# Another order table for a one-core attention and two-MLP kernel

## The chip, the cores and the metric

The kernel runs on one core of a Trainium2 chip. The metric is the device time of one launch in microseconds. Three runs of the kernel before give a median of 863.54 us (862.55 to 866.36).

## What is computed

Attention with two kinds of mask (a window of 32 keys for the first four heads, every fourth key of the last 128 for the others), and then two MLPs one after the other on its result, all in float32:

```python
def _attn_ref(q, k, v):                       # 4 batches, 8 heads, 576 positions, 64 wide
    scores = (1.0 / np.sqrt(D)) * np.matmul(q, k.transpose(0, 1, 3, 2))
    ...
    scores = np.where(masks[None, :, :, :], scores, -1000000000.0)
    scores = scores - np.max(scores, axis=-1, keepdims=True)
    attn = np.exp(scores)
    attn = attn / (np.sum(attn, axis=-1, keepdims=True) + 1e-09)
    return np.matmul(attn, v)

# x: 2304 tokens x 512; w_in 512 x 2048; w_out 2048 x 512; for both layers
x = np.square(np.maximum(x @ w_in, 0.0)) @ w_out
h = x @ moe2_w_in
x = (h * (1.0 / (1.0 + np.exp(-h)))) @ moe2_w_out
```

The weights come to the chip as 64-bit numbers and are made into pairs of float32 there: a high part that TensorE multiplies in its fast form, and the low remainder. Each product is three matmuls: high with high, high with low, low with high.

## The kernel before

The whole kernel is a list of about 4,000 steps (`Op`), each a few instructions of one engine or one transfer. `Kern` makes the steps: attention by half sequence and pair of heads (`attention`), the making of the weight pairs (`weights`), sums of weight blocks for a seven-product scheme (`sums`, `sums2`), the first layer on tokens in tiles of 256 (`mlp`) and 512 (`mlp2`), and the second layer in three tiles of 768 (`strassen`). Weights that are needed again go to device memory and come back by tile (`stream`, `stream2`).

What sets the order is one table, `ORDER`, from a search made ahead of time. It is a single list over all engines. A word names a step by its number, the engine that does it (P for TensorE, V for VectorE, A for ScalarE, G for GpSimd, D for a transfer, which SyncE issues), and behind @ the place of each buffer that the step takes. F words are dummy matmuls (`fill`). `Planner.order` emits the steps in that order, so an engine does its own words in the order in which they stand, and waits at a word until what it needs is there. A place holds 256 float32 columns of a ring in on-chip memory, or a bank of the accumulators; a step that takes a place waits until everything that used the place before it is done, a transfer out of it included.

Two places matter below. One is the chain by which a 512 KB piece of a second-layer weight is loaded and split (`weights`, lines 274 to 358): load `raw` (L274); on ScalarE, VectorE or GpSimd the steps `cv` (L282, L284) and `raw` (L290, L292); on VectorE or GpSimd the bit work on `cv` (L302 to L318), the high part and the remainder; store (L348, into `w2s`). The other is, in `strassen`, the split of a hidden tile into `hl` (L1169 high part, by ScalarE; L1171 remainder, by VectorE or GpSimd; both show as lines of the helpers `copy`, L245, and `sub`, L252) ahead of the TensorE steps at L1182.

A GpSimd step also waits, by a line in `run`, for the last VectorE step ahead of it in the list that reads two buffers of on-chip memory or is marked so (`lock`).

Of the kernel before, what the change touches and what calls it, by code (L numbers as in the profile page):

```python
# [10 lines left out]
F32 = mybir.dt.float32  # L11
# [1350 lines left out]
V113 D160@76 P86@2 V76 A154 V103 V77 V112 P104@1 A78@8 V110 V97 F8@3 V87 V114 V88 A105 V130 D169@80 A89 P115@1
V139 P106@0 A116 V131 P90@3 P117@2 D177@88 A91@60 V107 V140 A93@64 A132@68 F8@1 V118 V92 A144@10 G133 V94 V119
V108 P400@3@1@72@0 D186@92 A161@2 V109@12 A141@164 V120 G146 V403 F1@2 P121@0 V402 G142 V401 D506@201 A124 A122
V410 P404@2 A145 V123 V411 A153@14 V125 G399 V412 P1238@3 V147 D203@116 A405 A162 V155 V148 A179 P406@0 V156
D211@124 A149@84 P413@1 A1239@16 V407 V150 A1240 V163 A1241@6 P1244@3 D220@128 V157 A414 A171 V164 A158@168 V408
V1242 P415@2 A1245@18 V165 A409@8 P1243 V416 V159 A1246 A166@100 V417 V418 A170@0 D424@196 P507@0@1@96@1 V167
A1247@12 A178@4 V1248 P419@3 P1250@2 V510 A422@104 G172 A187@10 D194@108 V420 V508 V512 G180 A188 V525 V421
P1249 A511 G189 V523 V521 A1251@16 D228@36 V423 A522 V173 A513 V181 P426@3@0@112@2 A509 A526 V514 A1252 G174
F9@1 A196 V428 V429 V427 A195@6 V436 P430@2 V437 A524 V438 V515 V517 A516 A175@172 V527 P439@1 V182 A431 V425  # L1370
A1253@14 V528 V190 P432@3 A440 V176 A529 P518@0 A530 V1254 P441@2 V191 A183@120 P531@1 P1255 V433 V442 A192@176
V519 V533 G184 V434 A520 V443 V435@8 A532 A205 D539@196 V444 P534@3 A213 V204@2 V197 P445@0 P1256@1 V193 A446
A448 A537@12 V449 A535 V447 A212@0 V536 V198 A1257@18 D538 A1258 P540@0@3@20@3 D450@201 V199 A1259@4 A200@28
V1260 V558 P1261 A222 G206 V541 V556 D237@40 A557 V201 A559 V543 A542 P1262@1 V554 V207 A555 A544 D168 V545 V208
A546 P452@0@3@24@0 A1263@16 V560 V547 V451 V548 A1264 V561 V214 A563 D134 V562 F1@2 F2@1 V466 G550 A549 V455
P564@2 V454 V456 A565 V453 G209@180 A566 P551@1 V463 V465 D254@76 P457@2 A552 V464 A553 V215 A221@14 P567@1 V210
A1265@8 A458 V223 D245@72 P467@0 V1266 V224 P459@3 A468 V216 A568 D572@196 P469@2 A238@12 V460 V225 A217@32
P1267 V240 A229@10 V470 V461 G218 V462@6 A570@4 A230 V471 D478@201 V569 V472 A226@184 P473@0 V231 P1274@1 V227
A476@52 A474 A246@8 V475 D288@124 V477 V232 P573@3@0@56@1 A1275@18 V241 A1276 A239 V578 D271@112 V580 G233
P480@1@2@80@2 V576 V574 A1277@2 V587 V593 A577 V591 V589 A579 V1278 A575 D262@92 V242 A581 P1279 A590 V582 V482  # L1380
A234@88 V583 G479 V484 V481 G584 A592 V483 D571 V491 D305@24 A256 P485@0 V493 V492 V494 A594 V235 A588 P585@1
P495@3 A486 V595 V248 A255@6 D279@108 V272@0 P1286@0 A586 V596 V263@10 A243@188 V257 V597 A247 V249 A496 P487@2
A1287@16 V244 A1288 P598@1 P497@3 V488 V250 A599 A1289@2 P600@0 V489 V498 V1290 A490@14 V251@96 P1291 V499 V258
A603@4 A500 D605@201 V252 P501@2 V259 P1298@1 A502 A601 V504 D638@196 A260@192 G280@8 V505 V503 A273 V274
P1268@3 V265 A1299@18 V275 D296@116 A1300 V602 V261 P606@2@1@20@3 A1269@16 A307 V1270 P1280@0 G290 D219 V624
A264 V611 V613 G282 V609 D604 A1271@2 V622 V607 A1301@12 V266 P1292@3 A612 A610 V1302 A623 V267 A1281@18 V620
P1304@2 A1282 V1272 V268@128 A1283@14 V626 A621 V276 A614 P1273 A608 V269 A627 V1284 A1293@16 A625 V615 A1294
P1285 V628 V616 A298 V617 V629 A1295@6 V630 A277@132 V289@2 P618@0 A1305@18 P639@1@36@0 V278 A1306 A281 V619
P640@3 V643 A297@4 V641 V1296 P631@0 A1307@14 V652 P1310@2 V645 A653 V291 A632 V299 A646 V654 V283 A644 P633@0
A1311@16 V300 A642 P1316@1 A1312 V284 A1313@0 V656 A634 V636@10 A655 D666@201 V1308 P1297 A285@40 V635 V647 A657  # L1390
# [285 lines left out]
```

## Time and profile before

| what | value |
|---|---|
| median of three runs | 863.54 us |
| the profiled execution, its own time | 863.25 us |
| its span, first to last instruction | 861.5 us |
| TensorE busy | 844.4 us (98%) |
| VectorE, ScalarE, GpSimd busy | 675.9, 492.3, 169.6 us |
| 16 DMA engines, busy share | 74.2% |
| mean granted TensorE clock | 0.998 of 2.4 GHz |

The span is the profiled execution's; its time is 1.75 us longer. In the lists "L936" is a line of the kernel; PE is TensorE, PEld its weight loads, DVE VectorE, ACT ScalarE, POOL GpSimd, SP or SPq SyncE, which issues all transfers. "y<-hl,sw" is what is written and read.

### The profile page before, as it was taken

How to read it: one execution, taken by the hardware profiler on the slowest of the kernel's cores; microseconds unless marked ns; L12 is line 12 of the kernel's file. 1: busy time of each engine (PE TensorE's matmuls, PEld its weight loads, DVE VectorE, ACT ScalarE, POOL GpSimd, SP SyncE). 2: the span in 40 equal slices, each digit the busy share in tenths (PEclk: the TensorE clock that was granted, in tenths of full speed). 3: DMA queues.
4: the chain of work that ended last, by engine and by line, in shares of the span. 5: the costliest groups of instructions: out<-in, count | busy, mean ns of one | idle time of the engine just before them, and what ended most of it. 6: DMA issues, size and time to landing. Idle time of an engine off the chain costs nothing.

```text
span 861.5 us, 17083 instructions
## 1 busy us (share of the span) xinstructions
PE 844.4 (98%) x6029; PEld 797.8 (93%) x6029; DVE 675.9 (78%) x1733; ACT 492.3 (57%) x1288; POOL 169.6 (20%) x188
## 2 busy tenths in 40 slices
PE   8999999999999999899999999999999999999998
PEld 6879999999888988888988999999999999999998
DVE  5999999988887677567989999798815887537874
ACT  4989889877565364413432456675535565346552
POOL 3321000122204344123110221201200011101212
PEclk9999999999999999999999999999999999999999
DMA  9385678768989877778989899986686574682641
GB/s 340 149 273 173 201 248 275 278 227 306 360 287 328 315 276 267 261 267 300 341 292 352 310 347 309 341 284 236 233 306 233 195 256 173 215 296 89 220 148 74
DMA packets 83606, 223.59 MB, mean 260 GB/s; under 512 B 8768, under 2 KB 18240, under 8 KB 83520
## 3 DMA queue, kind: packets, MB, share of 16 engines
q1 hardware_dynamic: 83520, 222.49, 74.2%
q8 instruction: 48, 0.79, 0.4%
q14 instruction: 38, 0.31, 0.1%
HBM read 172.13 MB, written 50.33 MB: 258 GB/s over the span
## 4 chain that ended last, share of the span: by engine, by line
PE 84%; DMA 6%; DVE 4%; ACT 2%; issue 1%; POOL 1%; SPq 1%; ACTq 0%; POOLq 0%; DVEq 0%
PE y L1094 17%; PE sa L1182 14%; PE s L936 11%; PE y L1182 5%; PE y L991 4%; PE y L990 4%; PE y L992 4%; PE sa L1094 4%; PE s L788 2%; DMA w2s<-st 2%; PE ax L533 2%; PE s L790 2%; PE s L789 2%; PE y L836 2%; PE ax L625 2%; PE y L837 2%
## 5 line engine op out<-in xcount | busy, mean ns | idle before, releaser
L245 ACT CAST hl<-gq 128x384 fp32r<-128x384 f32 x168 | 79.0, 513 | 67.5 <-PE sa L1182 24.9
L1094 PE MATMUL y<-xs,ws 128*128 128x384 f32 x552 | 107.3, 334 | 0.0
L252 DVE TENSOR_TENSOR hl<-gq,hl 128x384 fp32r<-128x384 f32 x149 | 82.4, 581 | 23.2 <-ACT hl L245 22.5
L1094 PEld LDWEIGHTS y<-xs,ws 128*128 128x128 f32 x552 | 96.7, 188 | 0.1
L936 PE MATMUL s<-x,ws 128*128 128x256 f32 x576 | 78.5, 287 | 2.6 <-ACT ap L245 2.6
L1182 PE MATMUL sa<-hl,wp 128*128 128x384 f32 x432 | 79.6, 334 | 0.0
L936 PEld LDWEIGHTS s<-x,ws 128*128 128x128 f32 x576 | 74.1, 193 | 4.7 <-ACT ap L245 2.8
L991 PE MATMUL y<-g,w 128*128 128x512 f32 x192 | 75.4, 393 | 1.0 <-POOL g L252 1.0
L990 PE MATMUL y<-g,w 128*128 128x512 f32 x192 | 75.7, 394 | 0.0
L1182 PEld LDWEIGHTS sa<-hl,wp 128*128 128x128 f32 x432 | 75.3, 188 | 0.0
L992 PE MATMUL y<-g,w 128*128 128x512 f32 x192 | 74.9, 390 | 0.0
L1070 ACT COPY gq<-y 128x384 f32<-128x384 f32 x92 | 42.1, 478 | 55.4 <-PE y L1094 44.4
L952 DVE TENSOR_TENSOR h<-s,h 128x512 f32<-128x512 f32 x96 | 59.6, 620 | 17.3 <-PE s L936 9.8
L566 ACT ACTIVATE ap<-ap,ast 96x128 f32<-96x128 f32 (+3 forms) x168 | 62.2, 372 | 14.6 <-DVE ast L558 14.1
L245 ACT CAST g<-r 128x256 fp32r<-128x256 f32 (+1 forms) x82 | 41.1, 506 | 47.5 <-DVE r L972 27.3
L1065 DVE TENSOR_TENSOR gq<-y,gq 128x384 f32<-128x384 f32 x46 | 25.0, 553 | 47.8 <-PE y L1094 46.5
L252 POOL TENSOR_TENSOR hl<-gq,hl 128x384 fp32r<-128x384 f32 x19 | 24.5, 1297 | 190.4 <-ACT hl L245 124.1
L1133 DVE TENSOR_TENSOR gq<-gq,sg 128x768 f32<-128x768 f32 x48 | 47.6, 1004 | 12.0 <-ACT sg L1131 11.5
L788 PE MATMUL s<-x,w 128*128 128x256 f32 x192 | 56.3, 293 | 0.2
L790 PE MATMUL s<-x,w 128*128 128x256 f32 x192 | 54.3, 283 | 0.0
L789 PE MATMUL s<-x,w 128*128 128x256 f32 x192 | 54.2, 283 | 0.0
L1131 ACT ACTIVATE sg<-gq 128x768 f32<-128x768 f32 x48 | 40.3, 849 | 23.5 <-DVE gq L1065 13.6
(182 smaller groups left out, 2188.5 us busy)
## 6 DMA issues: line engine op xcount, KB each, us to landing
raw<-w SPq DMA_DIRECT2D x64, 512.0 KB, 5.5
ws<-w1x SPq DMA_DIRECT2D x48, 512.0 KB, 6.5
ws<-w2x SPq DMA_DIRECT2D x48, 512.0 KB, 5.9
sw<-w2y SPq DMA_DIRECT2D x48, 512.0 KB, 4.5
wa<-w1s SPq DMA_DIRECT2D x24, 512.0 KB, 6.7
wa<-w2s SPq DMA_DIRECT2D x24, 512.0 KB, 6.0
w1x<-st SPq DMA_DIRECT2D x16, 512.0 KB, 3.7
w2x<-st SPq DMA_DIRECT2D x16, 512.0 KB, 5.3
```

The costliest lines, as they stand in the source:

```text
L245: self.nc.scalar.copy(out=out, in_=in_)
L252: self.eng[eng].tensor_tensor(out=out, in0=a, in1=b, op=ALU.subtract)
L566: es.append(self.op({"ACT": c_act(nk) + 0.185}, lambda e, i=i, n=n, c=c, p=p, st=st: nc.scalar.activation(out=p.tile[:n, c], in_=p.tile[:n ...
L788: nc.tensor.matmul(o, wh.tile[:, s], xh, start=(kk == 0), stop=False)
L789: nc.tensor.matmul(o, wh.tile[:, s], xl, start=False, stop=False)
L790: nc.tensor.matmul(o, wl.tile[:, s], xh, start=False, stop=(kk == KC - 1))
L936: nc.tensor.matmul(bank.tile[:, o:o + 256], wp, xp, start=i == 0, stop=last, skip_group_check=True)
L990: nc.tensor.matmul(o, wh.tile[:, s], gh.tile, start=c == 0, stop=False)
L991: nc.tensor.matmul(o, wh.tile[:, s], gl.tile, start=False, stop=False)
L992: nc.tensor.matmul(o, wl.tile[:, s], gh.tile, start=False, stop=(c == NF - 1))
L1094: nc.tensor.matmul(o, w[part == 2].tile[:, kk * P:kk * P + P], x[b][part == 1].tile[:, kk * half:kk * half + half], start=new and not kk a ...
L1182: nc.tensor.matmul(o, u.tile[:, c * P:c * P + P], v.tile, start=new and not q and not part, stop=q == nf - 1 and part == 2, skip_group_che ...
```

## The change

Only the table differs. Every step that was there is there again; none is added. 338 of some 4,000 steps are done by another engine than before: 98 go from GpSimd to VectorE and 34 from GpSimd to ScalarE, 67 from VectorE and 18 from ScalarE to GpSimd, 66 from VectorE to ScalarE and 55 the other way. GpSimd has 123 steps in place of 170, VectorE 1,527 in place of 1,507, ScalarE 1,090 in place of 1,063. The dummy matmuls are 61 in place of 73. The 750 TensorE steps of the work and the 516 transfers are the same ones in another order. Its author describes the search: transfers land later in it, a transfer behind another one's landing is charged for it, and GpSimd instructions are longer.

Two lines of the table from the middle of the run, where the load of second-layer weight piece 11 (step 1795) stands, before and now (in the whole diff each line of the table differs):

```diff
-A2409@92 P2414@1 A1214 D2347@8 A1232 V1217 V2404@16 D1795@108 P2415@3 A2416@24 A2405@20 V2417 V1218 P2394 V2418
-D1782 A1219 V2419 V2406 D2304@96 V2410 A1797 V2420 D2356@72 P1220@0 P2429@1 V2425@18 A1221 A1796@6 P1233@2
+D2349@76 V1228 A1212 A1223 A1210 P2412@0 A1229 V1217 D1795@108 V1218 V1230 P2413@2 V1231 A2416@24 G2409@92 A1219
+D2348@100 P2414@1 V2417 D2305 P1220@0 V2418 P2415@3 V2419 D1782 V1232 P2429@1 V1784 D2346@120 P2407 V2410 V1797
```

On SyncE, around that load: `raw` with its buffer number is step 1795, and the two `w2s<-st` ahead of it are stores of pieces 9 and 10. Before:

```order
L660 DMA x1_1_70<-xo_5878 128x288
L348 DMA w2s_66<-st_5814 128x1024
L445 DMA wa_6081<-w1s_67 128x1024
L348 DMA w2s_66<-st_5992 128x1024
L445 DMA ws_6116<-w1x_68 128x1024
L445 DMA wc_6142<-w1s_67 128x512
L274 DMA raw_6153<-w2 128x512
L400 DMA w2x_73<-st_5738 128x1024
```

and now:

```order
L660 DMA x1_1_70<-xo_5890 128x288
L348 DMA w2s_66<-st_5998 128x1024
L348 DMA w2s_66<-st_5678 128x512
L868 DMA xr_6094<-x1_0_69 128x512
L660 DMA x1_2_71<-xo_6048 128x288
L445 DMA ws_6103<-w1x_68 128x1024
L445 DMA ws_6128<-w1x_68 128x1024
L274 DMA raw_6144<-w2 128x512
```

Before, the load stands third behind the store of `st_5992`, whose place, 108, it takes; now it stands sixth behind that store (`st_5998` there).

The first user of that load, with what stands behind it on the same engine. Before, on ScalarE:

```order
L245 CAST g4_6174<-r_6150 128x512
L590 ACTIVATE ap_6012<-ap_6012,ast_6013 72x104 x4
L290 ACTIVATE raw_6153<-raw_6153 128x512
L245 COPY ap_6012<-ax_6208 104x288
L282 ACTIVATE cv_6227<-raw_6153 128x512
```

and now, on VectorE:

```order
L252 TENSOR_TENSOR st_5748<-st_5748 128x512
L252 TENSOR_TENSOR g4_6167<-r_6123,g4_6167 128x512
L292 TENSOR_SCALAR raw_6144<-raw_6144 128x512
L247 COPY ap_6004<-ax_6191 104x288
L952 TENSOR_TENSOR h_6164<-s_6197,h_6164 128x512
```

The step moved from ScalarE to VectorE, and so did the copy out of an accumulator (step 1221) that stands right behind it in both; the TensorE step 2431 takes that accumulator next.

## Rows read from the trace of the kernel before

**Rows 1.** The page, busy time of each engine, share of the span, instructions.

```profile
PE 844.4 (98%) x6029; PEld 797.8 (93%) x6029; DVE 675.9 (78%) x1733; ACT 492.3 (57%) x1288; POOL 169.6 (20%) x188
```

**Rows 2.** Stretches: length, busy us of PE, PEld, DVE, ACT, POOL, clock, DMA share, GB/s.

```profile
0.00:20.00 20.00, 17.29 (x178) 13.67 (x178) 10.83 (x87) 8.66 (x29) 8.57 (x21) 1.00 0.92 333
20.00:80.00 60.00, 56.80 (x586) 51.49 (x584) 57.16 (x238) 55.07 (x168) 16.30 (x23) 1.00 0.66 224
...
200.00:360.00 160.00, 159.09 (x1285) 143.18 (x1283) 124.08 (x403) 85.84 (x302) 50.68 (x54) 1.00 0.86 298
360.00:400.00 40.00, 36.09 (x227) 31.80 (x225) 21.50 (x37) 8.82 (x17) 11.33 (x12) 0.96 0.86 298
...
500.00:700.00 200.00, 200.00 (x1140) 197.85 (x1139) 153.72 (x269) 113.03 (x219) 25.21 (x24) 1.00 0.77 272
700.00:720.00 20.00, 18.72 (x109) 18.40 (x108) 14.35 (x29) 10.61 (x23) 4.96 (x2) 1.00 0.66 220
```

**Rows 3.** The same view of one short stretch, behind the longest wait.

```profile
366.20:369.60 3.40, 3.40 (x28) 3.03 (x27) 2.37 (x5) 1.08 (x3) 2.20 (x2) 0.50 0.85 324
```

**Rows 4.** Waits of TensorE: who waited for whom, us in total, times, longest.

```profile
PE s L936 <- ACT ap L245: 2.6, 1, 2.6
PE y L1182 <- POOL hl L252: 1.3, 1, 1.3
PE y L991 <- POOL g L252: 1.0, 1, 1.0
...
PE s L936 <- DVE h L952: 0.9, 1, 0.9
PE s L936 <- ACT xo L245: 0.8, 1, 0.8
```

**Rows 5.** The chain of waits, 335 to 400 us: start us, us, what.

```profile
344.90 8.05 DMA w2s<-st
...
353.39 5.29 DMA w2s<-st
358.73 5.45 DMA raw<-w
364.28 0.15 ACT raw L290
...
364.84 0.39 ACT ap L245
365.27 2.19 PE s L936 x12
...
392.01 1.43 PE s L936 x12
...
393.44 0.23 PE y L990
```

**Rows 6.** ScalarE in order of time at 364 us, with the idle time before.

```profile
364.28 0.65 ACT L290 ACTIVATE raw<-raw 128x512 int32<-128x512 uint32 x1 [6.10 <-DMA raw<-w]
```

**Rows 7.** Waits of SyncE's queue for landings: us in total, times, longest.

```profile
SPq L445 <- DMA y<-yo: 17.6, 6, 5.1
...
SPq L445 <- DMA w2s<-st: 15.6, 4, 7.6
```

**Rows 8.** GpSimd and VectorE in order of time around 706 us, and GpSimd at 603 us.

```profile
706.79 4.00 POOL L252 TENSOR_TENSOR hl<-gq,hl 128x384 fp32r<-128x384 f32 x1 [33.48 <-DVE gq L252]
...
706.57 1.02 DVE L252 TENSOR_TENSOR hl<-gq,hl 128x384 fp32r<-128x384 f32 x2
...
709.38 0.55 DVE L252 TENSOR_TENSOR hl<-gq,hl 128x384 fp32r<-128x384 f32 x1
...
603.67 1.01 POOL L252 TENSOR_TENSOR hl<-gq,hl 128x384 fp32r<-128x384 f32 x1 [5.76 <-DVE hl L252]
```

**Rows 9.** The chain over the whole span, two pieces: start us, us, what.

```profile
0.99 5.31 PE fill L1248 x32
...
697.94 2.09 PE sa L1182 x12
```

More of the change, by code (lines that the diff above doesn't have):

```diff
@@ L1362 @@
[L1362 to L1366, printed above, removed]
@@ new lines @@
+D339@124 V1296 A285@40 P633@0 V278 A655 V299 P1297 A644 A634 D185 V647 V286 A294@136 A1307@14 V635 D666@201
+P1316@1 A1311@16 V306@6 A1312 V648 V658 A636@10 V659 V1308 A660 V295 P1322@2 D287 V1550@12 A649 D637 V308
+A1317@18 V1551@2 P661@0 A1313@0 P650@3 P1309 A662 V307 A315 V1314 V1552@112 A651 V324 A1318 P667@3@76@1
+V1554@108 A1323@16 V1553 A1324 V300 A1319@8 P663@1 A314@10 V669 P668@0 V1555 V673 A664@2 V1320 P1328@2 V682 V671
+V680 D694@196 A672 V684 V316 A674 P1334@3@0@1 V301 A670 A1329@18 V309 A302@72 D665 V675 A1330 P1315 V676 D253
@@ new lines @@
+D1609 V1610@12 P801@3 A1437@16 V378 P1411 A802 A803 A809 V1611@0 D1597 A1438 A805 V1614@76 P821@3@2@100@2
+A1427@14 V810 V1612@28 V811 P1423 A812 V822 G813 D1606 V824 A823 V826 V828 A825 V1428 A827 V839 P814@3 V835
+G1613 V837 P1429 A816 D1655@80 A829 V1615 A815 A1616 V841 V830 V831 A842 P817@3 V832 A1439@0 P833@2 V1440
+A818@12 V385 A840 P1442@3 A836 V1623@10 A838 A379@156 V843 V1617 D819 A1619 P1441 V844 D851@201 V845 A1443@18
+A834 V380 A1444 P846@2 V1622@14 P1448@3 A847 D1618 A1445@0 V1626@124 A392 V1624@20 V386 P848@2 A1449@16 V1625
@@ new lines @@
+V918 G1511@8 A907@6 V919 A923 V1512 V928 P920@2 D1539 V929 P1513 V930 D1537 A921 A1515@16 D908 V1516 D1670
+P931@2 V1684@8 P1520@3 A932 V1686 A1685 V1687 D936@201 P933@2 V2085 A1521@18 A1522 V1688 P2154@3 A934@6 A1523@4
+D2127@0 V1694@36 P2155@2 A1517@12 V2087 A2158@28 A1689@96 D967@196 V1692@116 V1518 P2156@3 V1524 V2159 V1690
+D935 P2157@2 D1702@20 V2160 V1693 V2161 P1519 V2162 D2133@80 V1695 V2170@18 P937@3@2@76@2 V2163@16 D1691
+A2171@32 P1525 A2164@120 G2172 D2130@24 V942 V940 V944 A941 V955 V938 A945 V951 V953 G2165 P2174@3 A952 V957
@@ new lines @@
+V1174@8 G2376 A1198 A1183 D2343@14 A1192 A1194 P2395@2 D1207@196 V2386 A1788 P2372 A1787@10 V1199 V1200 V1781
+P2373 V2387@16 D1766 P2396@1 V1789 A2388@36 V1186 V1201 A2399@24 V1790 P1202@0 D2337@28 P2377 V2391@18 V1203
+V1187 V1791 D2335@12 V1188 V2389 D2339@4 P1189@3 V2400 A1792@108 P1208@0@2@52@3 D2338@44 A1190 P1204@3 V1222
+V1793 D2342@112 P2397@1 A1205@2 G2392@48 G2393 P2398@3 D1175 V2401 D1794 V2402 V1209 P2390 V2403 D1775 V1224
+V1215 V1211 V2404@16 D2304@96 A2405@20 D1206 A1216 D2344@56 P2394 V2406 A1225 V1213 V1226 V2408@18 A1227 A1214
@@ new lines @@
+V2471 D1823@120 P2481@0 V2472@16 A2473@32 P2482@2 A2321@104 D1822 V2474 A2324@36 V1875 V2325 P2483@1 A1824@2
+V2476@18 A2484@96 V2322 A2318@112 D1896@72 P2462 V2485 A2477@28 G1826 A1825 V2486 A1876@203 D2541@64 V2487 V2478
+P2562@3 V2319 D2542@116 V1827 P2475 V2488 D1878@100 V2489@16 V1828 V2493@18 P2563@0 D2544@80 A2566@32 A2494@124
+A2490@20 P2564@2 A1897@14 V1832@56 D2540@108 V2495 A1880 V2491 A1898 P2565@1 V1833 D2534@68 V2567 A1836
+G1834@128 A1879@10 V2568 P2479 G1835 V2569 D2538@60 A1839 V2570 V1837 D2535@12 V1840 P2492 D2549@24 V1881
@@ new lines @@
+V2578@18 V2571@16 D1842@96 V1882 A2572@84 V1883 P2496 D1838 G1877 P2497 A2500@8 V2573 P2498 A2502@0 V1899
+A2579@20 P2499 A1884@199 D2501 P2582@3 V2506@4 A1829@88 P2583@0 D2503 A2586@100 V1830 D2546@28 V2504@2 P2574
+V1900 P2584@2 V1886@124 D1904@56 V2587 G1887 V1901 P2585@1 A1890 D2539@0 A1843@8 V2588 V1888@32 V2589 D1831
+G1845 P2599@3 V2590 G1889 D2505 P2600@0 A2603@40 A1902@197 V2591@16 D1841 A1906 A1893 G1891 P2601@2 V2604
+A1905@12 D2507 P2602@1 V2605 D2545@120 V2606 V2580 P2616@3 V1907 D2548@88 P2575 V1885 A2620@64 A2592@68 P2576
@@ new lines @@
+V2693@18 D2741@80 V2003 A2694@52 V1992@112 A1994 V2695 P2683 D2740@48 A1980@146 V1955 V2697@16 A2009@14 V1981
+A2698@88 V2011 D2745@84 A1988@142 V2521 A2010 P2696 V2699 A2785@60 D2748@56 V2004 V1993 V2012 D1851@64 V2005
+P2786@2 V2013 V2527 A2014@156 P2788 D2752@52 V1989 P2700 V2016@72 V2018@92 P2701 D2742@32 V2526 P2702 V2017
+P2790 V2706@4 A2708@6 D2749@68 A2528@172 V2015 P2703 V2787 A1853 P2792 V2529 D2026@24 A2710@10 A2789 P2794
+A2704@2 G2019 A2793@16 V2006@154 D2707 P2796 V2007 A2795@19 V1995 D2709 A1997 V1852@0 P2800@2 A2023 D2739@14
@@ new lines @@
+A2870@137 P2882 D2755@0 A2932@151 V2871 P2884 D2762@68 V2933 P2886 V2061@8 A2885@72 V2873 A2935@161 D2764@112
+V2062 A2883@63 P2890@0 V2936 A2878@137 V2887 G2063 P2892 V2881 G2964 V2891 P2894 V2879 D2766@98 P2898 V2064
+A2895 A2888@93 D2051 P2900 A2893 V2889 A2938@137 P2902 V2960 A2896@95 D2765@84 V2899 G2065 P2904 A2901@34
+D2759@4 P2908@3 V2897 D2763@2 V2939 A2941@95 P2910 V2070@56 A2903@37 V2068@76 A2948@187 V2905 P2934 V2909
+A2906@190 V2968 P2912 A2911 V2069 D2770@122 V2071 P2916 V2907 A2913 A2072 D2712@66 V2942 P2918 A2914@190 V2073
@@ new lines @@
+V3251 D3147 V3245 P3256 D3189@44 V3223 A3252@187 P3258 A3257 D3192@40 P3262 A3259 A3234@190 P3264 D3081 V3263
+D3188@96 V3253 P3266 V3235 P3268 D3193@48 A3267@37 A3260@187 P3272@2 V3269 A3265@34 A3242@190 P3274 V3273
+A3270@175 V3261 P3276 A3275 P3280 A3277 D3197@64 P3282 D3194@128 P3284 P3286 A3285@136 A3365@187 A3283@93
+P3290@0 V3287 V3281 P3292 V3255 D3198@104 V3243 P3294 G3366 D3196@124 P3298 A3295 A3293 V3387 A3288@172 P3300
+V3271 D3201@96 V3289 P3302 V3291 D3200@100 P3304 V3299 A3303@160 A3278@175 P3308@3 V3305 A3301@151 A3296@172
@@ new lines @@
+V3574 P3634 V3562 D3545 A3160@34 G3578 P3559 D3588@96 V3164 P3563 V3570 A3165@40 V3161 P3567 V3166 P3571
+D3595@120 V3167 P3575 V3163 A3633@16 D3481 A3635@19 P3636@1 D3547 G3168@46 D3591@68 P3638 G3169 P3579 A3639
+D3599@64 P3640 A3580@190 A3582 P3642 D3592@116 P3644 A3643@28 D3583 P3646 A3645@31 P3650@2 V3647 V3641 P3652
+D3602@100 P3654 D3598@128 P3658 A3655 A3653 P3660 V3659 D3581 D3596@124 P3662 A3661@52 P3664 A3663@61 D3603@96
+P3668@0 V3665 P3670 D3606@68 P3672 A3671 D3604@112 P3676 A3673 P3678 D3600@104 P3680 A3679@80 A3666@187 P3682
@@ new lines @@
+P3800 V3822 A3805@190 A3811@175 P3804 V3806 D3619@147 A3819@133 V3816 V3812 P3807 V3836 D3620@126 V3848 P3813
+A3808@190 V3830 A3809 V3844 P3817 A3823@130 V3820 D3621@113 A3831@175 V3824 A3827@187 P3821 A3837@139 V3828
+A3841@123 V3860 A3845@179 P3825 V3832 A3849@172 V3852 P3829 V3842 A3853@133 V3838 P3833 V3854 D3623@119 V3856
+P3839 V3846 A3834@176 A3857@187 G3850 P3843 A3870@139 A3861@130 V3858 P3847 G3864 P3851 A3876@179 V3871
+D3625@123 A3865@148 V3862 P3855 G3866 P3859 G3877 D3626@115 P3863 A3885@187 A3873@127 A3882@133 P3867 V3874
@@ L1609 @@
+P3939 A3955@161 V3953 A3963@148 V3932 P3942 A3967@139 V3930 V3956 P3945 V3990 D3933 V3970 P3948 D3931 V3968
+G3986 P3951 A3979@133 A3971@179 V3964 P3954 A3983@187 V3974 V3980 A3975@173 P3957 V3984 V3972 P3965 V3976
+A3991@161 P3969 A3987@176 P3973 V3988 P3977 V3992 P3981 V3960 V3958 P3985 P3989 P3993 P3996 D3959 P3997 D3961
+P3998 D3895 P3999 P4000 P4001 P4002 P4003 A3994@202 A4004 D3995 D4005
 """
```

436 lines of the change are left out of this document (191 added, 245 removed).

## The prediction

> **What bounds the kernel.** I read first how busy each engine is, then that by stretches of time, then who waited for whom, then the chain of waits, and last the queue of transfers. TensorE is busy 844.4 us of the 861.5 [rows 1], and its work is the same before and after, so all that another order can give lies in the 17.1 us in which it stands idle, and in time at a lower clock. The stretches say where this is [rows 2]: 2.7 us in the first 20, 3.2 from 20 to 80, 0.9 in the 160 from 200 to 360, 3.9 from 360 to 400, none from 500 to 700, 1.3 from 700 to 720. Behind the longest idle time the granted clock is at 0.50, the lower of the two levels (1.2 GHz), for 3.4 us, with TensorE busy all of it [rows 3]; work at half speed there costs at most 1.7 us. The list of waits names the single ones: 2.6 us for an accumulator copied by ScalarE, 1.3 and 1.0 for GpSimd, 0.9 and 0.8 for VectorE and ScalarE [rows 4].
>
> The longest wait has a cause that the chain shows [rows 5]. A store of a weight piece takes 8.05 us to land, the next store of that kind is held up and lands 5.29 us after its issue at 353.39, and only then, at 358.73, is the load of the next raw weight issued, because it takes the place of what the store reads. It lands 5.45 us later. ScalarE has stood at its first use for 6.10 us [rows 6]; right behind that use stands the copy that TensorE waits for. SyncE issues in order, so such a wait holds every transfer behind it; loads alone waited 17.6 and 15.6 us for two kinds of stores to land [rows 7].
>
> **The change, part by part.** I measure the distance between two words of the table by the TensorE work that stands between them, and call it room. Prices: twelve matmuls of 256 columns take 1.43 us, one of 512 columns 0.23, twelve of 384 columns 2.09 [rows 5, 9].
>
> *Transfers behind transfers.* In the load above, step 1795, two TensorE steps stand between the load and its first use before, P2415 (12 of 256) and P2394 (12 of 512): 1.4 + 2.8 = 4.2 us of room. Now six do, P2413, P2414, P1220, P2415, P2429, P2407: 1.4 + 1.4 + 0.2 + 1.4 + 0.7 + 2.8 = 8.0 us. The room from the store to the load that takes its place goes from 3.6 to 6.2 us; the stores there took 5.29 and 8.05. This is not one place: of the transfers that take a place out of which a store goes, 66 before and after, 18 had under 4 us of room and 5 have now, under 5 us it is 25 and 11, under 6 us 31 and 18. So fewer transfers start late, and SyncE's queue is held up less. What that is worth is read where it hurt, from 360 to 400: 3.9 us idle, of which 1.0 is the GpSimd wait below, and up to 1.7 of clock: 4.6 us. Bounds: nothing (the load of 8.0 us is still late) and all 4.6. I take 4.4, near the upper end, because 8.0 us of room stands against 5.45 for the landing, and leave 0.2, the idle share of the stretch before it.
>
> *GpSimd steps.* 47 fewer stay. The 1.0 us wait was for a remainder `g` that VectorE now makes, but the high part ahead of it still takes a place behind a store, with 2.8 us of room in place of 1.4 and a landing of over 5 us; I take half, 0.5, between 0 and 1.0. The 1.3 us wait was for a remainder `hl` with 2.1 us of room; it has 6.2 now. But in the second layer GpSimd makes 24 `hl` and not 19, and six of them have at most 2.1 us of room and a long row of VectorE steps behind them, against seven before, of which one cost 1.3. So 1.3 goes and 6/7 of 1.3, 1.1, comes: 0.2 gained, between 1.3 gained and 6.5 lost (five more like it).
>
> *The two small waits.* The 0.9 us wait follows a raw load with 2.8 us of room, now 3.6: half, 0.5. The 0.8 us wait is for a copy that takes a place behind a store with 3.1 us of room, and has the same 3.1 now: nothing. Steps of engines behind a store are hardly better off in general: under 5 us, 24 before and 23 now.
>
> *The start.* The first 80 us lose 5.9 us [rows 2], in the attention of the first heads, where TensorE waits for short chains of other engines. There 53 TensorE steps had a producer nearer than its own duration, 50 have now, and what is missing, each at the mean of its kind, falls from 23.4 to 20.4 us, by 13%: 0.8 gained, between 3.0 gained and 2 lost. The 12 dummy matmuls less cost nothing: at 5.31 / 32 = 0.17 us each [rows 9] they are 2.0 us, but they stand where TensorE waits anyway. If nothing covered them, 2.0 would be gained.
>
> *More work on VectorE.* It has 20 steps more, about 0.55 us each [rows 8], 11 us. Most land where it has time (200 to 400). In the first 50 us of TensorE work, though, it gets 4.9 us more, each step at the mean of its kind, and it is busy 57.2 of 60 there [rows 2]; in the next 50 it has 3.2 less. Bounds 0 and 4.9; I take 0.8, nearer the lower end, as the added steps replace results of GpSimd that it waited for.
>
> Sum: 4.4 + 0.5 + 0.2 + 0.5 + 0.8 - 0.8 = 5.6 us off the profiled execution's 863.25: 857.7 us. That execution lies 0.3 us below the median of the three runs.
>
> **Rivals.**
>
> *A stall of the same kind at another place.* The search makes all rooms anew, and where one step of an in-order engine stands at a load that is late, the price is that of the one above, 4.6 us. For it: of loads that go straight to TensorE 9 now have under 4 us of room, and 4 had. Against it: the counts behind stores above. One such stall: 857.7 + 4.6 = 862.3, no change.
>
> *VectorE becomes the bound at the start.* All 4.9 us show in place of the 0.8: 861.8, no change. For it is its 95% busy share from 20 to 80; against it that GpSimd has 6 us less there, whose results VectorE waited for.
>
> *GpSimd is shut out by VectorE.* The GpSimd step at 706.79 took 4.00 us where the same shape took 1.01 at 603.67; VectorE began a row of steps with two on-chip inputs 0.2 us ahead of it, and GpSimd ended 0.9 us after the last of them at 709.93 [rows 8]. If each of the six `hl` steps with little room were held so, at the 1.3 us of the one, the sum would lose 6 x 1.3 - 1.1 = 6.7 us: 864.4, no change. Against it: before, one of seven was. The Trainium skill, SBUF — State Buffer, section Who interferes with whom, has it as a rule that a VectorE instruction with two SBUF inputs and a GpSimd instruction that reads SBUF exclude each other, and that whichever is issued first keeps the shared port. By that rule all six are held when VectorE's row runs without a gap; the 4.00 us row agrees, the 1.01 us row shows that a gap is common.
>
> *The first use of a raw load stops an engine more often (slower).* The load is late, the engine that splits it stands, and a copy for TensorE stands behind it. Raw loads with at most 3 us of room are 6 now and were 4. Each full case costs 2.9 us of idle time and up to 1.7 of clock, 4.6. One takes back most of the gain; from three on, 13.8 - 5.6 = 8.2, it is slower: 871.4. Against it: those with under 5 us are 13 and were 21, and the four with 3 us before cost TensorE 0.9 us and a part of the stretch from 360 to 400.
>
> *The table's room is not what the chip has.* SyncE issues ahead of the table's place when it can, so more room there may not start a transfer earlier; then nothing of the 4.4 comes: 862.1.
>
> **How the numbers follow.** Chances: the forecast 0.50, a stall elsewhere 0.14, VectorE 0.10, GpSimd shut out 0.06, no room in fact 0.08, raw loads slower 0.12. A measurement of this kernel can tell about 0.5%, 4.3 us, from no change. The forecast's own range is 853 to 860.5 (3 us more gained at the start and 1 us in GpSimd's waits; 2.8 less at either), and a small part of it is within 0.5%. So faster 0.47, same 0.40, slower 0.13. The range takes in the cases of no change with a mishap more and leaves out the slowest: 852 to 867.
>
> **What would show it.** Right: no store behind a store in the chain around 340 to 360; TensorE idle under 1 us and the clock at 1.00 from 360 to 400; less waiting of SyncE for landings than in [rows 7]; GpSimd busy about 130 us in place of 169.6. Wrong: a wait of TensorE over 2 us for ScalarE or VectorE behind a `raw` load, a GpSimd `hl` step of 3 us or more with TensorE waiting, or VectorE busy 60 of 60 us from 20 to 80 with more TensorE idle time than 3.2.

## The result, and the profile after

The changed kernel takes 852.88 us, the median of four runs (851.85 to 857.24); the kernel before takes 864.86 beside it (862.55 to 866.36). The ratio is 0.9873, 95% interval 0.983 to 0.9917: faster by 1.3%, some 12 us, where the forecast was 857.7, about half of that gain. The profiled execution took 851.85 us, its span is 850.0.

In some runs of many of the kernels here the mean clock is below 0.996 and the time 4 to 5 us longer (the changed kernel's 857.24 us, at 0.992, is one; the traces of e1 and e7 show the clock at half for 14 and 10 us near the start), so beside the median of all runs stands that of the runs at 0.996 or more, called runs at full clock.

The page after, busy time of each engine and the chain's shares, answers to [rows 1], and behind them the chain's shares of the page before:

```profile
PE 839.9 (99%) x6017; PEld 795.9 (94%) x6017; DVE 681.7 (80%) x1754; ACT 501.2 (59%) x1322; POOL 122.2 (14%) x142
...
PE 93%; ACT 3%; issue 1%; DVE 1%; POOL 1%; POOLq 0%; ACTq 0%
```

```profile
PE 84%; DMA 6%; DVE 4%; ACT 2%; issue 1%; POOL 1%; SPq 1%; ACTq 0%; POOLq 0%; DVEq 0%
```

The span fell by 11.5 us: TensorE's idle time from 17.1 to 10.1, and its busy time by 4.5. In the latter are the 12 dummies (0.11 us each at full clock, 1.3 us) and up to 1.7 us of the stretch at half clock; the rest, 1.5, I can't place. No transfer is left among the shares of the chain, where transfers had 6%. The stretches of [rows 2], with the short one of [rows 3]:

```profile
0.00:20.00 20.00, 17.75 (x182) 14.11 (x183) 11.89 (x91) 9.34 (x34) 5.21 (x15) 1.00 0.92 340
20.00:80.00 60.00, 56.87 (x584) 52.18 (x583) 58.34 (x247) 57.34 (x181) 10.51 (x12) 1.00 0.72 244
200.00:360.00 160.00, 160.00 (x1283) 143.68 (x1282) 130.85 (x413) 85.83 (x296) 26.82 (x36) 1.00 0.89 308
360.00:400.00 40.00, 40.00 (x268) 36.25 (x267) 30.73 (x49) 15.61 (x30) 10.64 (x10) 1.00 0.87 293
500.00:700.00 200.00, 198.96 (x1147) 198.41 (x1146) 150.18 (x265) 114.05 (x225) 29.36 (x26) 1.00 0.77 269
700.00:720.00 20.00, 20.00 (x117) 20.00 (x116) 18.16 (x36) 11.53 (x23) 2.03 (x2) 1.00 0.52 176
```

```profile
366.20:369.60 3.40, 3.40 (x25) 3.18 (x24) 1.12 (x3) 1.10 (x3) 1.57 (x2) 1.00 1.00 376
```

TensorE has no idle time left from 200 to 400 us and from 700 to 720, and the clock stays at 1.00, its upper level of 2.4 GHz. From 500 to 700 it has 1.04 us of idle time, where it had none. That is a new wait, the longest of TensorE's list, which answers to [rows 4]:

```profile
PE y L1094 <- ACT gq L1070: 1.0, 1, 1.0
PE fill L1248 <- DVE warm L1240: 1.0, 1, 1.0
PE y L836 <- ACT g L245: 0.8, 1, 0.8
```

ScalarE in order of time shows what it is: the copy of `gq` that TensorE wants stands behind a table load of 1.28 us and three more steps.

```profile
507.06 0.48 ACT L1070 COPY gq<-sa 128x384 f32<-128x384 f32 x1 [2.64 <-PE sa L1094]
507.56 1.28 ACT L1131 ACT_TABLE_LOAD   x1
508.85 0.85 ACT L1131 ACTIVATE sg<-gq 128x768 f32<-128x768 f32 x1
509.60 0.60 ACT L245 CAST st<-st 128x512 fp32r<-128x512 f32 x1
510.11 0.66 ACT L290 ACTIVATE raw<-raw 128x512 int32<-128x512 uint32 x1
510.68 0.83 ACT L1070 COPY gq<-y 128x384 f32<-128x384 f32 x2
```

SyncE's list of waits for landings, which answers to [rows 7]; the three longest lines:

```profile
SPq L274 <- DMA w2y<-st: 7.4, 2, 5.7
SPq L274 <- DMA w1x<-st: 7.1, 3, 3.8
SPq L445 <- DMA w2s<-st: 4.8, 2, 2.9
```

All lines of that kind together are 62.6 us in 48 waits, and were 133.0 in 58. Around raw piece 11, in order of time on SyncE, and its first use on VectorE, which answers to [rows 6]:

```profile
343.60 1.48 SPq L348 DMA_DIRECT2D w2s<-st  x2
...
347.24 0.36 SPq L274 DMA_DIRECT2D raw<-w  x1
```

```profile
358.24 0.42 DVE L292 TENSOR_SCALAR raw<-raw 128x512 int32<-128x512 uint32 x1
358.57 0.45 DVE L247 COPY ap<-ax 104x288 f32<-104x288 f32 x1
```

The load was issued at 347.24 (before: 358.73, [rows 5]), 11 us ahead of the step that uses it, and VectorE came to that step without idle time. It was not that transfers had become quick: this load took 8.3 us to land (before: 5.45), and so it had landed 2.7 us ahead of its use. GpSimd has no long `hl` step left where [rows 8] had one of 4.00; around there:

```profile
707.31 1.01 POOL L252 TENSOR_TENSOR hl<-gq,hl 128x384 fp32r<-128x384 f32 x1 [2.85 <-DVE hl L252]
...
725.44 1.58 POOL L252 TENSOR_TENSOR hl<-gq,hl 128x384 fp32r<-128x384 f32 x1 [1.05 <-DMA ws<-w2x]
```

**Where the 11.5 us come from.** I set the start of each TensorE step against the TensorE work ahead of it in its table (each step at a fixed time for its kind) and call the difference its lateness. What the changed kernel is less late, by stretches of that work: 1.7 us over the first 300, and 1.3 for the dummies that it does not do; 6.1 from 340 to 380; 1.2 from 380 to 500; 1.35 lost at the new wait; 0.5 from 510 to 680; 1.6 near 690 to 700 (GpSimd's `hl`); 0.4 behind that. Over half is the one stall.

### The profile page after: what moved, and what is told of

Its sections match the earlier page's. It is cut to its first block, busy times and chain, and to the rows that moved or that the text cites. A ratio compares the mean times of both kernels' runs of the same rounds, so it can differ in the third digit from the quotient of the medians.

```text
span 850.0 us, 17035 instructions
## 1 busy us (share of the span) xinstructions
PE 839.9 (99%) x6017; PEld 795.9 (94%) x6017; DVE 681.7 (80%) x1754; ACT 501.2 (59%) x1322; POOL 122.2 (14%) x142
## 4 chain that ended last, share of the span: by engine, by line
PE 93%; ACT 3%; issue 1%; DVE 1%; POOL 1%; POOLq 0%; ACTq 0%
PE y L1094 17%; PE sa L1182 15%; PE s L936 14%; PE y L1182 6%; PE y L990 5%; PE y L991 5%; PE y L992 5%; PE sa L1094 4%; PE s L788 3%; PE s L789 2%; PE s L790 2%; PE ax L533 2%; PE y L836 2%; PE ax L625 2%; PE y L837 2%; PE y L838 2%
## 5 line engine op out<-in xcount | busy, mean ns | idle before, releaser
L252 DVE TENSOR_TENSOR hl<-gq,hl 128x384 fp32r<-128x384 f32 x144 | 78.7, 580 | 17.7 <-ACT hl L245 14.5
L936 PE MATMUL s<-x,ws 128*128 128x256 f32 x576 | 76.3, 284 | 0.0
L936 PEld LDWEIGHTS s<-x,ws 128*128 128x128 f32 x576 | 72.3, 191 | 1.2
L245 ACT CAST g<-r 128x256 fp32r<-128x256 f32 (+1 forms) x86 | 42.9, 504 | 50.8 <-DVE r L972 42.2
L1182 PE MATMUL y<-hl,sw 128*128 128x384 f32 x288 | 51.4, 334 | 0.0
L1182 PE MATMUL sa<-hl,sw 128*128 128x384 f32 x288 | 50.9, 334 | 0.0
```

What stands on the lines that cost most here:

```text
L245: self.nc.scalar.copy(out=out, in_=in_)
L252: self.eng[eng].tensor_tensor(out=out, in0=a, in1=b, op=ALU.subtract)
L936: nc.tensor.matmul(bank.tile[:, o:o + 256], wp, xp, start=i == 0, stop=last, skip_group_check=True)
L1182: nc.tensor.matmul(o, u.tile[:, c * P:c * P + P], v.tile, start=new and not q and not part, stop=q == nf - 1 and part == 2, skip_group_che ...
```

## The experiments

The words of a table can be moved, and two tables can be spliced: each step takes the same places in both, so a table may run in the order of one as far as some step, and go on with what is left in the order of the other. "Loss" is the lateness that comes in between 340 and 380 us of TensorE work, in the profiled execution; it is 6.4 us before and 0.3 after.

| kernel | median of all runs, us (range, runs) | ratio to before, 95% interval | runs at full clock, median | loss |
|---|---|---|---|---|
| before, 60 runs beside these | 863.46 (859.64 to 871.28) | 1 | 41, 862.48 | 6.4 |
| after | 852.88 (851.85 to 857.24, 4) | 0.9873, 0.983 to 0.9917 | 3, 852.82 | 0.3 |
| e1, copy first | 863.91 (858.36 to 869.32, 12) | 0.9996, 0.997 to 1.0022 | 8, 862.80 | 6.2 |
| e2, store first | 861.24 (856.98 to 863.07, 12) | 0.9956, 0.9936 to 0.9975 | 9, 859.62 | 2.8 |
| e3, engines alone | 873.19 (871.97 to 873.93, 6) | 1.0096, 1.0074 to 1.0117 | 6, 873.19 | 3.3 |
| e4, order alone | 879.11 (878.67 to 879.72, 4) | 1.0166, 1.014 to 1.0192 | 4, 879.11 | 0.3 |
| h1, start alone | 863.30 (859.40 to 871.23, 12) | 0.9995, 0.9961 to 1.003 | 9, 862.93 | 5.1 |
| h2, 300 to 380 alone | 857.13 (856.23 to 864.31, 10) | 0.9933, 0.9899 to 0.9966 | 7, 857.10 | 0.3 |
| h3, from 300 on | 856.21 (853.95 to 864.97, 12) | 0.9946, 0.9916 to 0.9976 | 9, 855.76 | 0.3 |
| e5, one `hl` on VectorE | 863.05 (1) | one run | 1, 863.05 | |
| e6, stores back | 852.55 (851.56 to 854.29, 6) | 0.9878, 0.9849 to 0.9906 | 6, 852.55 | 2.2 |
| e7, no dummies | 855.62 (854.67 to 858.01, 6) | 0.9913, 0.9884 to 0.9942 | none | 0.3 |
| e9, back to ScalarE | 854.72 (1) | one run | 1, 854.72 | 0.3 |
| b1, mended | 851.85 (851.10 to 854.98, 6) | 0.9855, 0.9818 to 0.9892 | 6, 851.85 | 0.3 |

**Is it the word order on the engine, or the load? (e1, e2)** Two single words of the table of before, moved. First the copy that TensorE waited for, set ahead of the step that stood at the load:

```diff
-V2410 A1797 V2420 D2356@72 P1220@0 P2429@1 V2425@18 A1221 A1796@6
+V2410 V2420 D2356@72 P1220@0 P2429@1 V2425@18 A1221 A1797 A1796@6
```

> The kernel before with one word of its table moved: ScalarE's first pass over raw piece 11 (step 1797) goes behind the copy that frees the accumulator (step 1221) instead of ahead of it. The raw piece lands as late as before. Theory 1 (one late transfer, with an engine's queue stopped behind it, makes the stall, and the half clock follows from the stall): the wait of 2.6 us of TensorE for ScalarE's ap copy and the 3.4 us at half clock go, 4 to 6 us off the kernel before, ratio 0.993 to 0.995. Rival (the stall only moves, since what hangs on the late piece waits as well): under 1.5 us off, ratio 0.998 or more.

The rival was right. ScalarE in order of time, and TensorE:

```profile
370.05 0.65 ACT L290 ACTIVATE raw<-raw 128x512 int32<-128x512 uint32 x1 [4.29 <-DMA raw<-w]
...
371.44 0.38 ACT L950 COPY h<-s 128x256 f32<-128x256 f32 x1
```

```profile
371.86 0.72 PE L625 MATMUL ax<-ap,blk 104*64 104x72 f32 x16 [2.61 <-ACT h L950]
```

ScalarE makes its copy, stands at the load all the same, and a copy of `h`, the third step behind it, is what TensorE waits for: 2.61 us in place of 2.6, and the half clock behind it as well. The loss is 6.2 where it was 6.4. (The whole execution is late by 5 us because its clock had fallen at the start, see below.) Then the store, set ahead of a load that waited for another store's landing:

```diff
-A1229 D2342@112 A1783 A1225 V1784 V1213 V2403 D1794 P2412@0
+A1229 D1794 D2342@112 A1783 A1225 V1784 V1213 V2403 P2412@0
```

> The kernel before with one word moved: the store to w2s (step 1794), behind whose landing the load of raw piece 11 is issued, goes ahead of the load (step 2342) that stood before it in SyncE's queue and waited 8 us there for the landing of another store. ScalarE's order is left as it was. Theory 1 (a transfer behind a transfer): the store leaves about 8 us earlier, at 345 us and not 353, raw piece 11 is issued at about 353 us instead of 358.7 and has landed before ScalarE comes to it at 359 to 361; stall and half clock go, 4 to 6 us off, ratio 0.993 to 0.995. Rival (the store waits for its own data, or the raw load for something else than that store): raw piece 11 is issued after 357 us and the ratio is 0.998 or more.

SyncE in order of time, ScalarE at the load, and two of TensorE's waits:

```profile
346.51 4.11 SPq L348 DMA_DIRECT2D w2s<-st  x2
353.61 0.32 SPq L445 DMA_DIRECT2D wa<-w1s  x1
...
354.99 0.38 SPq L274 DMA_DIRECT2D raw<-w  x1
```

```profile
362.23 0.67 ACT L290 ACTIVATE raw<-raw 128x512 int32<-128x512 uint32 x1 [2.40 <-DMA raw<-w]
```

The second store is off by 350.6 us, so that its landing falls into SyncE's wait for the first. It isn't off at 345 as expected, since it waits 3.3 us for its own data from GpSimd (the rival's point, in part). The raw load leaves 3.7 us earlier than before, not 5.7, and took 7.1 us to land; ScalarE still stood 2.40 us, but TensorE did not wait for it. Of the 2.8 us of loss that are left, TensorE's list has 0.6 for a later transfer, which took 7.68 us to land, and 0.9 for the `g` of GpSimd that the kernel before waits for as well:

```profile
PE y L991 <- POOL g L252: 0.9, 1, 0.9
...
PE s L936 <- DMA wa<-w1s: 0.6, 1, 0.6
```

So one word of SyncE's queue gives back 3.6 of the 6.4 us in the trace, 2.9 at full clock (862.5 to 859.6), less than the 4 to 6 expected, and one word of ScalarE's gives back nothing.

**Order or engines? (e3, e4)** The table of before with the letters of the changed one, and the other way round. Eight words of e3:

```diff
-P531@1 P1255 V433 V442 A192@176 V519 V533 G184
+P531@1 P1255 V433 V442 A192@176 V519 A533 V184
```

> The kernel before in its own order, with each step on the engine that the changed table gives it (338 steps change engine, GpSimd has 80 steps fewer than before). Theory 1 (the order and its room make the gain, mostly at one stall): the stall around 365 us is still there, GpSimd's 4 us step at 707 us is gone; 0 to 2 us off, and a loss of up to 3 us is possible because the steps were placed for other engines; ratio 0.997 to 1.004. Rival (fewer steps on GpSimd make the gain): 5 us or more off, ratio 0.994 or less.

> The changed kernel's order with each step on the engine that it had before. Theory 1 (the order makes the gain): most of the changed kernel's gain stays, 6 to 11 us off the kernel before, ratio 0.987 to 0.993, and SyncE's long waits for landings (15 us and more a source line) are gone. Rival (fewer steps on GpSimd make the gain): under 4 us off, ratio 0.995 or more.

(GpSimd has 47 steps fewer with the changed letters; the 80 in the first expectation is a slip of mine.) Neither theory had it: each half of the change alone is slower than no change, by 8 and 14 us in the ratio. In e3 the late `hl` step is there again, in another shape, two steps in 6.82 us, but most of its loss lies ahead of 250 us of TensorE work (9.8 us by lateness). The stall is there in part: with the load's first use on VectorE, VectorE stands at it for 4.50 us and TensorE waits 2.5 us for an `h` of VectorE, without the half clock.

```profile
712.35 6.82 POOL L252 TENSOR_TENSOR hl<-gq,hl 128x384 fp32r<-128x384 f32 x2 [19.06 <-DVE hl L252]
```

In e4 the stall is gone and SyncE waits 64.3 us for landings, as little as in the changed kernel. It loses most of its time in the first 360 us: 70.42 busy us of the first 80 where the changed kernel has 74.62, 116.66 of the 120 behind them (119.87), and 155.41 of the 160 from 200 us on (160.00). First e4, then the changed kernel:

```profile
0.00:80.00 80.00, 70.42 (x692) 60.95 (x693) 64.39 (x302) 57.89 (x182) 25.57 (x42) 0.97 0.72 250
```

```profile
0.00:80.00 80.00, 74.62 (x763) 66.29 (x764) 70.24 (x337) 66.68 (x214) 15.71 (x27) 1.00 0.77 268
```

So SyncE's waits are no measure of the time by themselves (h2, below, gains most of what the change gains with 111.4 us of them), and a gain can't be split into "order" and "engines": a step's place in the list fits the engine that does it.

**Which part of the list? (h1, h2, h3)** Splices. A few of the words that h1 (the first pair) and h2 (the second, from the middle of its piece) take from the changed table, against those of before:

```diff
-V1 G0 F32@0 D64@144 D3@140 D2@132 D33@136 G4
+V1 G0 F32@0 D3@140 D2@132 D33@136 V4 D64@144
...
-A2409@92 P2414@1 A1214 D2347@8
+D2349@76 V1228 A1212 A1223
```

h1 takes all as far as 60 us of TensorE work, h2 those from 300 to 380 us, h3 all from 300 us on.

> The changed table's words as far as 60 us of TensorE work, and from there the table of before (steps that the first part already holds are left out of the second): the start alone of the change, with its 12 fewer dummy multiplies. Theory 1 (lateness read against TensorE's work done in the two traces: the start is worth 1.6 us, 1.3 of it dummies): 1 to 2.5 us off the kernel before, ratio 0.997 to 0.999, and the stall of 2.6 us near 365 us still there. Rival (the gain is spread evenly over the table): the first 7 per cent of the work carry under 1 us, ratio 0.999 or more. Rival (the start is the main gain): over 4 us off, ratio 0.995 or less.

> The table of before as far as 300 us of TensorE work, the words of the changed table from there to 380 us, and the table of before again behind them: the stretch with the stall alone. Theory 1 (over half of the gain is this one stall, and it hangs on the order of stores and loads there): 4.4 to 6.1 us off the kernel before, ratio 0.993 to 0.995, TensorE without a wait of 2 us between 340 and 380 us. Rival (the gain is spread over the whole table): under 2 us off, ratio 0.998 or more.

> The table of before as far as 300 us of TensorE work, and the words of the changed table from there to the end. The piece from 300 to 380 us alone gave 857.1 us in seven of ten runs. Theory 1 (what is left of the gain lies in a few places: GpSimd's late step near 707 us worth 1.6 us, a smaller wait near 740 us worth 0.4, less the new wait of 1.2 to 1.3 us near 510 us, and in the first 300 us of the work): 855 to 857 us in runs at a clock of 0.998 or more, so that the first 300 us carry 2.5 to 4 us of the rest. Rival (all of the rest is behind 380 us): 852 to 854 us.

h2 is what theory 1 said: the stretch alone gives 5.4 of the 9.7 us at full clock, and these runs lie within 1 us of each other, where those of before spread over 7. Its stretch in the profile:

```profile
360.00:400.00 40.00, 40.00 (x271) 36.29 (x270) 30.55 (x51) 11.80 (x23) 11.91 (x11) 1.00 0.87 305
```

h3 falls in the middle of what was expected: what lies behind 380 us gives 1.3 more (857.1 to 855.8), and the first 300 us the last 2.9 (855.8 to 852.8). h1 shows nothing of these 2.9, 862.9 against 862.5, but it has a wait of 2.1 us for an attention load at 63.6 us, just behind the seam, that neither of the two tables has; whether the first 60 us carry 1.6 us, as the lateness says, stays open.

**GpSimd's late step (e5).** One letter:

```diff
-A3477@125 G3466 D3214@77 P3461
+A3477@125 V3466 D3214@77 P3461
```

> The kernel before with one letter changed: the subtraction hl (step 3466) that took GpSimd 4.00 us at 707 us goes to VectorE, in its place in the order. Theory 1 (GpSimd gets no turn beside VectorE's row of steps with two inputs, so this step ended last): TensorE's wait of 1.3 us for hl goes and the stretch of 20 us from 700 us on has 20.0 us of busy TensorE instead of 18.7; VectorE does the step in 0.5 to 1.1 us. Rival (TensorE waits for the data ahead of hl, whatever engine subtracts): a wait of over 0.8 us stays there. The whole time can't tell 1.3 us in one look; the stretch does.

```profile
700.00:720.00 20.00, 20.00 (x117) 20.00 (x116) 16.23 (x33) 11.52 (x25) 1.21 (x1) 1.00 0.68 231
```

The 20 us from 700 on are full, and the wait for `hl` is off TensorE's list; by lateness it cost 1.6 us. The whole time of one run, 863.05 us, can't show that.

**Undoing the change in the changed kernel (e6, e9).** The two stores put back directly ahead of the loads that take their places:

```diff
-D1766 P2396@1
+P2396@1
...
-V1793 D2342@112
+V1793 D1766 D2342@112
...
-V2401 D1794 V2402
+V2401 V2402
...
-V1217 D1795@108
+V1217 D1794 D1795@108
```

> The changed kernel with the two stores of its stretch put back where the table of before has them on SyncE's queue: step 1766 directly ahead of the load 2342 that takes its place, step 1794 directly ahead of the load of raw piece 11 that takes its place. Theory 1 (two waits for landings in a row, some 5 us each, used up SyncE's lead): SyncE's two waits come back with 3 to 8 us each, and raw piece 11 is issued 3 to 6 us later than the 347.2 us of the changed kernel, at 350 to 353 us; it lands by 359 us, and the table here asks for it at about 360.7 us, so TensorE barely waits: 0 to 1.5 us slower than the changed kernel, 853 to 854.5 us. Rival (the place of these two stores is the whole of the stretch's gain): the stall of 2 us or more and the half clock come back, 4 to 6 us slower, 857 to 859 us.

The list of SyncE's waits from 325 to 370 us, and the chain of waits there:

```profile
SPq L274 <- DMA w2s<-st: 7.1, 1, 7.1
SPq L445 <- DMA w2s<-st: 6.9, 1, 6.9
```

```profile
348.06 7.68 DMA w2s<-st
...
355.80 5.28 DMA raw<-w
...
361.52 0.45 DVE ap L247
361.97 0.61 DVE h L952
...
362.62 3.14 PE s L936 x24
```

Both waits are back and the load is issued at 355.80, 8.6 us later than in the changed kernel and not 3 to 6; the landing is again at the head of the chain. It costs TensorE 1.2 us there, 1.9 over the stretch in this execution, and nothing in the median (852.55). The clock did not fall. So these two stores are not the whole of it. Of the 8.6 us, 3.0 go because the load lands in 5.28 us and not in 8.3, and 2.7 are the time for which the landed piece had lain unused in the changed kernel; VectorE comes to it 2.9 us later (361.18 us), some 0.7 of which this execution was late already at 300 us. And the piece back on ScalarE, with the copy behind it as before:

```diff
-V1797 V1221 G1796@6
+A1797 A1221 G1796@6
```

> The changed kernel with the pass over raw piece 11 (step 1797) and the copy behind it (step 1221), which it has on VectorE, on ScalarE in that order, as before. Theory 1 (the load had landed, so no engine stops there): TensorE has no wait of over 0.8 us between 340 and 380 us, the time is within 1 us of the changed kernel. Rival (taking these steps off ScalarE's queue made the gain): a wait of 2 to 3 us of TensorE for ScalarE is back, and some time at half clock.

```profile
358.67 0.68 ACT L290 ACTIVATE raw<-raw 128x512 int32<-128x512 uint32 x1 [1.63 <-DMA xr<-x]
```

ScalarE waited for another load there, not for the raw piece, and TensorE is busy 40.00 of the 40 us from 360. With e1 this settles that the engine of that step was not the cause. (It is 1.9 us slower than the changed kernel's runs at full clock. That lies ahead of 70 us, in a wait of 1.6 us of TensorE for ScalarE at 64 us and 2 us at half clock, where nothing was edited.)

**The dummies (e7).** All fillers behind the first 32 taken out:

```diff
-F5@2
...
-F2@2
```

> The changed kernel without its 29 dummy multiplies behind the first 32 (about 0.11 us each, 3.1 us of TensorE work; they compute nothing that is kept). Theory 1 (they lie in time in which TensorE waits for VectorE and ScalarE, as the prediction had it, and their use is the clock): in runs at full clock the time is that of the changed kernel within 1 us, and more runs have half clock between 11 and 25 us (4 to 5 us longer, mean clock 0.994 or less): more than half of them, where the kernels so far had it in about one of three. Rival (they cost their time): 2 to 3 us off at full clock.

The stretches from 20 to 28 us and on:

```profile
20.00:28.00 8.00, 7.08 (x50) 6.48 (x50) 6.17 (x26) 6.45 (x17) 2.51 (x2) 0.50 0.66 270
28.00:32.00 4.00, 4.00 (x29) 3.89 (x27) 3.49 (x9) 2.83 (x8) 0.00 (x0) 0.72 0.00 0
```

Every one of the six runs had the half clock (mean clock 0.986 to 0.994), and with 3.1 us less work the kernel is 2.7 us slower in the median. As no run at full clock is among them, whether the dummies cost anything there was not told apart; what they do here is hold the clock.

**Mending the new wait (b1).** The copy of `gq` set ahead, and five dummies in a wait of 0.64 us at 10 us:

```diff
-P2808 A2805 D2746@96 A2798@161 P2810 A2020 V2799 A2028 D1999 P2812 V1856 A2803 A2811@28
+P2808 A2803 A2805 D2746@96 A2798@161 P2810 A2020 V2799 A2028 D1999 P2812 V1856 A2811@28
...
-V48 P13@0
+V48 F5@1 P13@0
```

> The changed kernel with two words edited: ScalarE's copy of gq (step 2803), for which TensorE waits 1.0 us near 510 us behind a table load and three other ScalarE steps, goes ahead of the gq copy in front of that load; and five more dummy multiplies stand in TensorE's wait of 0.64 us at 10 us. Theory 1: the wait near 510 us goes, 1.0 to 1.3 us off the changed kernel, about 851 us, ratio to the kernel before 0.984 to 0.987. In some executions of every kernel so far the clock fell to half between 11 and 25 us and cost 4 to 5 us (mean clock 0.994 or less); if idle time at 8 to 12 us starts that, it comes in none or one of the runs here, where it came in about one of four. Rival (the wait moves to the next step of ScalarE, and the dummies push the start later): no faster than the changed kernel, 852 to 853 us.

```profile
PE y L1094 <- ACT gq L1070: 0.6, 1, 0.6
```

The wait near 510 us is gone, and one of the same kind, 0.6 us, has come at 529 us: half of it moved. 851.85 us is 1 us below the changed kernel's median, which these runs can't tell from nothing; at full clock it is 851.85 against 852.82. None of six runs had the half clock, but none of e6's six had it either, which has not these five dummies; so these runs don't show that they help. (Not every kernel so far had the half clock, as the expectation says: none of the ten runs of e3 and e4 is below 0.996.)

## Why the prediction was right, and where its sizes were off

**The place and the mechanism were right.** The stall behind the load of piece 11 was the largest term, its cause was transfers behind transfers (one store's place gives 2.9 us of it in e2, all the places and engines of the stretch 5.4 in h2; how the rest divides is open), and what I named as its signs came: no store in the chain, no idle time from 360 to 400, clock at 1.00, SyncE's waits halved, GpSimd busy 122.2 us.

The size was off by half: 852.88 us lies just below the forecast's own range of 853 to 860.5, and inside the outer one by 0.9 us. What that range allowed at its lower end came, about 3 us more at the start and 1.4 at GpSimd's `hl`, and the stall gave more besides.

**Transfers, 4.4 forecast, 6.1 in the trace and 5.4 by h2.** With the 0.5 of the `g` wait it was 4.9. The step that failed is the upper bound of 4.6: I added up TensorE's idle time and the clock, less the `g` wait, between 360 and 400 us. The loss of the whole stretch is 6.4, and all of it went, `g` too.

**The room as a price** was the weaker part. I argued from 8.0 us of room against 5.45 for a landing. That step failed, and the term came all the same, in part by luck: the load took 8.3 us to land, more than its room, and was in time because SyncE issued it 11.0 us ahead of its use, 3 more than the room. e6 issues it 8.6 us later, and TensorE waits only 1.2 us for that. And e4 has the changed table's order, SyncE's waits as short as its own, and is 14 us slower than before. My counts of rooms (18 and 5, 31 and 18) told the direction of SyncE's waits, not of the time. The rival that the table's room is not what the chip has was wrong as to the result, and half right in that: SyncE did issue ahead of the table's place.

**GpSimd's `hl`, 0.2 forecast, 1.6 measured.** That the 4.00 us step was the cause, e5 shows. The step that failed is "6/7 of 1.3 comes": none of the `hl` steps with little room made TensorE wait near there. In the changed kernel they took 1.01 to 1.61 us; before one took 4.00, in e3 two took 6.82. Which of them meets a row of VectorE steps without a gap was the open part, and I took it at an average. The Trainium skill (SBUF — State Buffer, Who interferes with whom) has the rule that a VectorE instruction with two inputs in this memory and a GpSimd instruction that reads it exclude each other; the long rows agree with it, and e5 shows what it cost here.

**The small waits, 0.5 forecast, 2.0 in the trace**: 1.1 for `h`, 0.9 for `xo`, which I had costed at nothing. The first is hardly a term of the change: in the profiled executions of e2, h1 and h2, whose words there are those of before, lateness is 0.9 to 1.1 less at that place as well. The second is one: e1, e2, h1, h2 and h3, which have the words of before there, wait 0.3 to 1.5 us for `xo`, and the changed kernel does not.

**Start 0.8, VectorE -0.8**: the first 300 us gave 2.9 (h3 to the whole), and the two terms come to nothing together. VectorE's added work left no trace: from 20 to 80 us it is busy 58.34 and not 57.16, and TensorE is idle 3.13 us, not 3.20. The 12 dummies less I had costed at nothing, as TensorE waits there anyway, and their work at 0.17 us each, from the first 32; where they stand it is 0.11. Whether their 1.3 us of work came back as time stays open with h1; what the step left out is that dummies hold the clock (e7).

**Not forecast**: the new wait near 510 us, 1.35 us. Nothing in my counts looked at what ScalarE has ahead of a `gq` copy.

By places, what came beyond the forecast: 3.0 us in the first 300 (0.9 of it the `xo` wait, 1.3 the dummies' work), 1.2 at the stall, 0.7 at `h` and near it, 1.4 at `hl`, 0.9 at two places behind 510, less 1.35 at the new wait: 5.85 us, which with the 5.6 of the sum make the 11.5 of the two spans.

## What to carry to other kernels

When a load waits behind a store's landing, look at what holds the *store* in its queue: two stores side by side wait once, with a load between them twice; moving one word there was worth 2.9 us, and moving the copy ahead of the step that stood at the load nothing, as a step behind it stood there as well. A table of order and the engine of each step are one thing; testing half of such a change tells only that they belong together, while splicing it by time tells where its gain lies. And counts of slack over a whole table say little until the one place where TensorE waits has been found.

## What the runs showed of the hardware

TensorE's clock near the start hangs on little. From 8 to 11.3 us TensorE was busy 2.23 us in the profiled execution of e1 and 2.18 in that of the kernel before, which has the same words there; in e1 the clock then went to its lower level, 1.2 GHz, for 14 us, in the kernel before it stayed at 2.4. First e1, then the kernel before (length, PE busy, clock, DMA share, GB/s):

```profile
8.00:10.00 2.00, 1.42 (x22) 1.00 0.99 378
10.00:12.00 2.00, 1.46 (x11) 0.84 1.04 355
12.00:14.00 2.00, 2.00 (x14) 0.50 0.99 379
```

```profile
8.00:10.00 2.00, 1.34 (x22) 1.00 0.99 376
10.00:12.00 2.00, 1.54 (x15) 1.00 1.01 283
12.00:14.00 2.00, 1.80 (x18) 1.00 0.98 370
```

Of the kernel before 19 of 60 runs were below a mean clock of 0.996, of h2 three of ten, of e7, with less to do there, all six. Their median is 4.6 us above that of the others for the kernel before, nearly as much as the stall that the change removed. Behind the stall the clock hangs on as little: it fell behind waits of TensorE of 2.6 us in the profiled executions of the kernel before and of e1 and of 2.5 in that of e5, and stayed at 1.00 behind one of 2.5 in e3 and one of 1.9 in h1. And landings are no constant against which room can be set: a store of 512 KB to `w2s` took 8.05 us in the kernel before and 3.5 in the changed one (the one issued at 343.60), where the load of piece 11 behind it took 8.3 and not 5.45, with the DMA engines 0.97 and not 0.80 busy from 335 to 366 us.
